# Second to fourth 512 rows of a down projection as seven half-size fp16 products, in a fused gated-attention kernel

## The chip, the core and the metric

One core of a Trainium2 chip runs the whole program. The metric is the device time of one execution in microseconds (us). Engines run their own instruction streams in order and meet through semaphores: TensorE (PE, with its weight loads PEld), VectorE (DVE), ScalarE (ACT), GpSimd (POOL) and SyncE (SP, which issues most DMAs).

## What is computed

```python
xn = layernorm(x)                                   # x: 2048 x 640
s  = windowed attention over the last 512 cached keys: 32 heads of 192, then @ wo
h  = sigmoid(xn @ w_gate) * (xn @ w_up)             # 640 -> 1536
g  = silu(h @ w_down)                               # 1536 -> 640, the down projection
out = x + s * g
```

The inputs are bf16. The change concerns `h @ w_down` and the silu behind it.

## The kernel before

**Stage B** comes first. It takes the 2048 rows in four groups of 512 (`s` = 0 to 3, L457). In each, `f` runs over the 12 blocks of 128 of the hidden size: ten matmuls of 512 columns give gate and up in the two banks of one PSUM pair (L469), ACT takes the sigmoid of the gate bank (L474), and DVE multiplies it with the up bank into `hT_sb[:, f, :]` (L475). Then the down projection takes the four row tiles `q` of 128: for every `f` a matmul of 512 columns and one of 128 with the same weights (L517), accumulated over the 12 blocks in one pair; ACT takes the sigmoid (L524), DVE multiplies (L525), POOL stores the tile `gB_sb` to `gB_d` (L541). PSUM is used as four pairs of banks that `bank2` (L79) hands out in turn, so a pair is free again when the group four steps back has been read.

**The other work of stage B** is put between these steps and runs in the order of the source, since the schedule is manual (L34). On DVE: layer norm statistics and normalization of the next 512 rows (L344, L349, L359); the sums of inputs for the query products (`sum_x`, L438 to L452); the scan of `wq` for its largest magnitude, sixteen pieces, each an `and` and a `max` (`scan_fold`, L199); the reduction to a scale (`set_scale`, L207), whose row maxima go to DRAM and come back on all partitions (two POOL DMAs), and `set_scale2` (L212), which waits for them. On ACT, in `s` = 3: the scaling of raw query weights to fp16 (`scale_raw`, L237) and copies (`copy_w`, L247); `sum_w` (L255) puts four DVE operations and one ACT copy in line, the copy waiting for DVE's second operation.

**Attention** follows (L548 on). Its first query products (`query_slots`, L579; L729) use PSUM banks 2 and 3, then 4 and 5, then 0, 1 and 6. The attention output goes through the output projection at the end, which already has the seven-product form (`product`, L933; `sum_op`, L706; `sum_quad`, L778): each 2x2 block product is made of seven products of half size and of sums before and after, where ACT copies partial results out of PSUM (`keep`, L944) and DVE adds (L957) or gates them (L921).

Of the kernel before, what the change touches and what calls it, by code (L numbers as in the profile page):

```python
# [17 lines left out]
def kernel(  # L18
# [14 lines left out]
    P = 128  # L33
# [53 lines left out]
    def flat(ps):  # L87
        return ps.rearrange("p b n -> p (b n)")
# [40 lines left out]
    w_sc = const.tile([P, 10], F32, name="w_sc")  # L129
# [141 lines left out]
    with ExitStack() as bctx:  # L271
# [3 lines left out]
        hpool = bctx.enter_context(tc.tile_pool(name="hpool", bufs=2))  # L275
# [14 lines left out]
        wmax = bone.tile([P, NCD, NSC], BF16, name="wmax")  # L290
        mx_row = bone.tile([P, P], F32, name="mx_row")
        x_tiles = {}

        def load_x(t):
            x_sb = xin_pool.tile([P, D], BF16, name=f"x_sb{t}")
            nc.sync.dma_start(x_sb[:], xf[t * P:(t + 1) * P, :])
            x_tiles[t] = x_sb[:]
# [157 lines left out]
        folds = {(0, 9): 0, (0, 10): 1, (0, 11): 2, (2, 0): 11, (2, 1): 12, (2, 2): 13, (2, 4): 14, (2, 5): 15}  # L455
        folds_q = {(0, q): 3 + q for q in range(TQ)} | {(1, q): 7 + q for q in range(TQ)}
        for s in range(NST):  # L457
            hT_sb = hpool.tile([P, NF, 512], BF16, name="hT_sb")
            pi = s // 2
            if s % 2 == 1:  # L460
                sw = swap(pi)
            for f in range(NF):
# [12 lines left out]
                nc.vector.tensor_tensor(hT_sb[:, f, :], gu[:, 1, :], sig_sb[:], ALU.mult)  # L475
# [11 lines left out]
                if (s, f) in folds:  # L487
                    scan_fold(wmax, folds[s, f])
                if s == 1 and f < NSB:
# [5 lines left out]
                elif s == 2 and f == 6:  # L495
                    set_scale(wmax[:].rearrange("p c n -> p (c n)"), mx_row)
# [16 lines left out]
            for q in range(TQ):  # L513
                oB_ps = flat(bank2())
                for f in range(NF):
                    for d0, dsz in d_chunks:
                        nc.tensor.matmul(  # L517
                            oB_ps[:, d0:d0 + dsz], lhsT=hT_sb[:, f, q * P:(q + 1) * P],
                            rhs=wd_sb[:, f, d0:d0 + dsz],
                            start=(f == 0), stop=(f == NF - 1),  # L520
                        )
                gB_sb = gpool.tile([P, D], BF16, name="gB_sb")
                sg = bone.tile([P, D], F32, name="sg")
                nc.scalar.activation(sg[:], oB_ps[:, 0:D], AF.Sigmoid)  # L524
                nc.vector.tensor_tensor(gB_sb[:], oB_ps[:, 0:D], sg[:], ALU.mult)  # L525
                if (s, q) in folds_q:
                    scan_fold(wmax, folds_q[s, q])
                if s == 3:
                    if q == 0:
                        scale_w(0, NCD - 1)  # L530
                    elif q < 3:
                        scale_raw(1, q - 1)
                    if q == 1:
                        sum_w(0, NCD - 1)
                        load_raw(1, 2, nc.gpsimd)
                    if q < 3:
                        sum_x(pi, 3 + q, sw)
# [531 lines left out]
```

## Time and profile before

| | |
|---|---|
| median of 3 runs | 881.0 us (880.94 to 881.07) |
| profiled execution | 881.17 us |
| its span in the profile | 879.4 us |
| PE busy | 872.0 us (99% of the span) |
| DVE / ACT / POOL busy | 670.0 / 577.2 / 231.6 us |
| L517, the down projection | 384 matmuls, 4 blocks of 13.04 us |
| granted TensorE clock in the first 220 us | 1.00 |

How to read it: the busy share of an engine is an average over stages with different limits. The chain of work that ended last follows the run back from its last instruction, at each step to what released it; in order of time it gives the start and length of each stretch. The lists of one engine in order of time give start, busy time, line, operation and operands, and in brackets the idle time before and what ended it. In the groups by form, the numbers behind the bar are the busy time in us, the mean ns of one, and idle time with what ended it.

### The profile page before, as it was taken

The numbers are of one execution on the slowest core, as the hardware profiler recorded it, in microseconds if no ns is written. First come the engines' busy times: TensorE is split into PE (matmuls) and PEld (weight loads), VectorE is DVE, ScalarE is ACT, GpSimd is POOL, SyncE is SP. The second block draws the span as 40 slices with busy tenths as digits, with TensorE's granted clock in tenths as the row PEclk, the third lists the DMA queues.
The fourth block names the chain that finished last, engine by engine and source line by source line (L and its number), as shares of the span: only waits on it lengthen the run. The fifth ranks groups of instructions, "written<-read, shape, count | busy, mean of one in ns | idle before, by whom it ended". The sixth has DMA issues, their size and how long they took to land.

```text
span 879.4 us, 18793 instructions
## 1 busy us (share of the span) xinstructions
PE 872.0 (99%) x7605; PEld 564.0 (64%) x7605; DVE 670.0 (76%) x1088; ACT 577.2 (66%) x693; POOL 231.6 (26%) x326
## 2 busy tenths in 40 slices
PE   9999999999999999999999999999999999999998
PEld 5445454557757757757757757757757777777775
DVE  4879947677767767767767767768877768888986
ACT  4323347765887887887797797786484666666662
POOL 0050212582344344334334334334000000000000
PEclk9999999999999999999999999999999999999999
DMA  9994465328698998898989898789997798557641
GB/s 273 268 276 113 107 117 123 93 56 156 163 218 143 197 215 151 178 225 150 196 210 143 200 213 154 147 193 215 215 272 137 203 367 267 181 168 267 193 138 38
DMA packets 246935, 161.34 MB, mean 183 GB/s; under 512 B 158848, under 2 KB 231808, under 8 KB 246848
## 3 DMA queue, kind: packets, MB, share of 16 engines
q1 hardware_dynamic: 238304, 132.90, 62.1%
q0 software_dynamic: 8544, 27.24, 14.4%
q8 instruction: 59, 0.97, 0.5%
q14 instruction: 28, 0.23, 0.1%
HBM read 93.65 MB, written 30.41 MB: 141 GB/s over the span
## 4 chain that ended last, share of the span: by engine, by line
PE 97%; ACT 1%; DVE 1%; DMA 0%; issue 0%; SPq 0%; DVEq 0%
PE ps_all L571 20%; PE ps_all L938 20%; PE ps_all L671 20%; PE ps_all L657 19%; PE ps_all L469 11%; PE ps_all L517 6%; PE ps_all L382 1%; ACT E L661 0%; DMA x_sb<-in_A_x_dram 0%; ACT qp L590 0%; DVE arm L921 0%; DVE arm L967 0%; ACT mid L720 0%; DVE arm L965 0%; DVE qT L605 0%
## 5 line engine op out<-in xcount | busy, mean ns | idle before, releaser
L661 ACT ACTIVATE E<-ps_all 128x1024 bf16<-128x1024 f32 x256 | 251.6, 1021 | 122.8 <-PE ps_all L657 122.1
L657 PE MATMUL ps_all<-qT,kT 64*128 64x512 bf16 x1536 | 197.7, 376 | 0.4 <-ACT E L661 0.3
L671 PEld LDWEIGHTS <-E 128*128 128x128 bf16 x2048 | 169.5, 98 | 9.9 <-issue 9.8
L671 PE MATMUL ps_all<-v_sb,E 128*128 128x193 bf16 x2048 | 174.9, 247 | 0.0
L605 DVE TENSOR_TENSOR qT<-ps_all,qp 128x512 bf16<-128x512 f32 x176 | 116.9, 687 | 47.5 <-PE ps_all L571 39.9
L592 DVE COPY qp<-ps_all 128x512 f32<-128x512 f32 x150 | 100.6, 687 | 48.0 <-PE ps_all L571 48.0
L657 PEld LDWEIGHTS <-kT 64*128 64x128 bf16 x1536 | 83.8, 94 | 80.2 <-issue 6.0
L678 DVE TENSOR_TENSOR o_st<-ps_all,rden 128x768 bf16<-128x768 f32 x128 | 122.5, 957 | 4.4
L938 PEld LDWEIGHTS <-mid 128*128 128x128 f16 x996 | 97.4, 98 | 37.8
L571 PE MATMUL ps_all<-mid,arm 64*128 64x512 f16 (+1 forms) x840 | 105.7, 376 | 0.0
L571 PE MATMUL ps_all<-mid 64*128 64x512 f16 (+1 forms) x840 | 104.5, 376 | 0.6 <-ACT qp L590 0.5
L571 PEld LDWEIGHTS <-mid 64*128 64x128 f16 x840 | 47.8, 94 | 45.0 <-issue 2.2
L571 PEld LDWEIGHTS <-arm 64*128 64x128 f16 x840 | 47.9, 94 | 43.8 <-issue 0.3
L774 ACT ACTIVATE mid<-mid,w_sc 128x1536 f16<-128x1536 bf16 x41 | 63.5, 1572 | 0.0
L971 POOL DMA_DIRECT2D out_dram<-arm x14 | 7.6, 542 | 196.3 <-DVE arm L967 196.3
L240 ACT ACTIVATE mid<-mid,w_sc 128x1536 f16<-128x1536 bf16 x37 | 58.2, 1572 | 0.6
L226 POOL DMA_DIRECT2D mid<-in_A_wq_dram x80 | 48.2, 608 | 23.9 <-DVE mid L262 22.4
L474 ACT ACTIVATE sig_sb<-ps_all 128x512 bf16<-128x512 f32 x48 | 28.0, 596 | 40.1 <-PE ps_all L469 37.1
L517 PE MATMUL ps_all<-wd_sb,hT_sb 128*128 128x512 bf16 (+1 forms) x384 | 52.8, 299 | 0.0
L938 PE MATMUL ps_all<-arm,mid 128*128 128x320 f16 x348 | 51.0, 299 | 0.0
L475 DVE TENSOR_TENSOR hT_sb<-ps_all,sig_sb 128x512 bf16<-128x512 f32 x48 | 32.5, 682 | 22.8 <-PE ps_all L469 11.7
L938 PE MATMUL ps_all<-op,mid 128*128 128x320 f16 x336 | 48.2, 299 | 0.0
(160 smaller groups left out, 1046.2 us busy)
## 6 DMA issues: line engine op xcount, KB each, us to landing
oT_d<-oT SPq DMA_DIRECT2D x64, 384.0 KB, 5.1
mid<-oT_d SPq DMA_DIRECT2D x45, 384.0 KB, 4.7
mid<-in_A_wq_dram POOLq DMA_DIRECT2D x80, 192.0 KB, 6.7
arm<-in_A_wo_dram SPq DMA_DIRECT2D x16, 480.0 KB, 5.7
v_sb<-in_A_v_cache_dram SPq DMA_DIRECT2D x28, 192.0 KB, 6.0
kraw<-in_A_k_cache_dram SPq DMA_DIRECT2D x26, 192.0 KB, 4.2
mid<-in_A_wq_dram POOLq DMA_DIRECT2D x9, 480.0 KB, 7.1
kT<-oT_d SPq DMA_DIRECT2D x11, 384.0 KB, 4.5
```

The lines of the kernel that those rows point to most:

```text
L240: nc.scalar.activation(raw.bitcast(F16), raw, AF.Copy, scale=w_up)
L469: nc.tensor.matmul(gu[:, i, :], lhsT=w[:, c, f * P:(f + 1) * P], rhs=xnT[s][:, c, :], start=(c == 0), stop=(c == NCD - 1),)
L517: nc.tensor.matmul(oB_ps[:, d0:d0 + dsz], lhsT=hT_sb[:, f, q * P:(q + 1) * P], rhs=wd_sb[:, f, d0:d0 + dsz], start=(f == 0), stop=(f == NF ...
L571: nc.tensor.matmul(ps_all[:, b, :], lhsT=w(r, c), rhs=x[r, c, :], start=(first and k == 0), stop=(k == len(cs) - 1), skip_group_check=True,)
L592: nc.vector.tensor_copy(dst, part(b))
L605: nc.vector.tensor_tensor(q_out(i, u, pp), part(b), t, ALU.add)
L657: nc.tensor.matmul(ps[:, b, :], lhsT=kT[h, c * PC + j, :], rhs=qT_t[r][i, j][h, pp, :], start=(j == 0), stop=(j == PC - 1),)
L661: nc.scalar.activation(E_t[r, i, pp][:, c, :, :], ps, AF.Exp, scale=scale_qk)
L671: nc.tensor.matmul(o_ps[:, q // 2, q % 2, 0:DH + 1], lhsT=E[:, c, h, q * P:(q + 1) * P], rhs=vt[:, c, 0:DH + 1], start=(c == 0), stop=(c = ...
L678: nc.vector.tensor_tensor(o_st[:, :, h * DH:(h + 1) * DH].rearrange("p (b i) d -> p b i d", b=2), o_ps[:, :, :, 0:DH], rden[:].to_broadcas ...
L774: eng.activation(t, t.bitcast(BF16), AF.Copy, scale=v_up)
L938: nc.tensor.matmul(ps_all[:, b, d0:d1], lhsT=a[:, c, :], rhs=w[:, c, d0:d1], start=(start and c == 0), stop=(c == KB - 1), skip_group_chec ...
```

## The change

`s` = 0 keeps its down projection. For `s` = 1 to 3, `down7` replaces the loop over `q`. h and `w_down` are held as fp16, scaled by powers of two. h is split in two halves of the hidden size and two pairs of row tiles, `w_down` in two halves of the hidden size and `LEFT` and `RIGHT` columns; for each of the two tiles of a pair, seven products of six matmuls of 320 columns are formed. Their operands need three new sums of `w_down` and one in place, made once (`sum_wd`), and three sums of h and one in place for every 512 rows (`sum_h`). Partial results are kept by ACT (`keep`); `gate` adds, takes the sigmoid with the joint scale undone and multiplies.

The scales come from bounds: ACT sums magnitudes (`Abs` with an accumulated output) of `w_up` (`scan_h`) and `w_down` (`scan_wd`), DVE takes the largest and cuts it to a power of two (`bound`), and a matmul with the identity spreads it over the partitions (`bound2`). `scan_abs` does so for pieces 7 to 15 of `wq`, in place of `scan_fold`.

`hT_sb` has one buffer instead of two. The first four x tiles are loaded into `h_sums`; `wmax` and the scans' output lie in the tiles of the `w_down` sums. What stood between the row tiles of `s` = 3 is now called from `after_down`.

```diff
-        hpool = bctx.enter_context(tc.tile_pool(name="hpool", bufs=2))
+        hpool = bctx.enter_context(tc.tile_pool(name="hpool", bufs=1))
...
+        NH = NF // 2
+        assert NSC * NCD == NH * DN and NH * DN == 3 * D
+        wd_sums = [bone.tile([P, NH, DN], F16, name=f"wd_t{n}") for n in range(3)]
+        h_sums = bone.tile([P, 3, NH, 2 * P], F16, name="h_sums")
+        halves = bone.tile([P, 8, DN], F32, name="halves")
+        wmax = wd_sums[1][:].bitcast(BF16).rearrange("p a b -> p (a b)").rearrange("p (c n) -> p c n", c=NCD)
+        scan_out = wd_sums[2][:].bitcast(BF16).rearrange("p a b -> p (a b)")
...
+        mx_b = bone.tile([P, P], BF16, name="mx_b")
+        scans = bone.tile([P, 20], F32, name="scans")
...
+        x_first = h_sums[:].bitcast(BF16).rearrange("p a b n -> p (a b n)")
...
+        def scan_abs(i):
+            nc.scalar.activation(scan_t[i], scan_t[i], AF.Abs, accum_out=scans[:, i - NSB + 1:i - NSB + 2])
+        def scan_h(k):
+            v = wu_sb[:, :, 3 * k * P:3 * (k + 1) * P]
+            nc.scalar.activation(
+                scan_out.rearrange("p (c n) -> p c n", c=NCD), v, AF.Abs, accum_out=scans[:, 10 + k:11 + k])
+        def scan_wd(k):
+            v = wd_sb[:, 3 * k:3 * (k + 1), :]
+            nc.scalar.activation(
+                scan_out.rearrange("p (c n) -> p c n", c=3), v, AF.Abs, accum_out=scans[:, 14 + k:15 + k])
+        def bound(mx, at):
+            nc.vector.tensor_reduce(mx, scans[:, at:at + 4], axis=mybir.AxisListType.X, op=ALU.max)
+            nc.vector.tensor_scalar(mx, mx, 1e-30, None, op0=ALU.max)
+            bits = mx.bitcast(I32)
+            nc.vector.tensor_single_scalar(bits, bits, 0x7F800000, op=ALU.bitwise_and)
+            nc.vector.tensor_copy(mx_b[:], mx.to_broadcast([P, P]))
+        def bound2(mx, ps, up, down, k):
+            nc.tensor.matmul(ps, lhsT=mx_b[:], rhs=ident[:], start=True, stop=True)
+            nc.vector.tensor_reduce(mx, ps, axis=mybir.AxisListType.X, op=ALU.max)
+            nc.vector.tensor_scalar(down, mx, k, None, op0=ALU.mult)
+            nc.vector.reciprocal(up, down)
...
+        def scale_wd(k):
+            v = wd_sb[:, 3 * k:3 * (k + 1), :]
+            nc.scalar.activation(v.bitcast(F16), v, AF.Copy, scale=wd_up)
+        def sum_wd(n):
+            B11, T1, T2, B21, T3, B22, T4 = wd_ops
+            a, b, c = ((T1, T3, B11), (T2, B22, T1), (T3, B22, T3), (T4, B21, T2))[n]
+            nc.vector.tensor_tensor(a, b, c, ALU.subtract)
+        def sum_h(h16, j0, j1):
+            A11, A21, A12, A22 = (
+                h16[:, k * NH + j0:k * NH + j1, i * 2 * P:(i + 1) * 2 * P] for k in range(2) for i in range(2))
+            S1, S2, S4 = (h_sums[:, n, j0:j1, :] for n in range(3))
+            tt = nc.vector.tensor_tensor
+            tt(S1, A21, A22, ALU.add)
+            tt(S2, S1, A11, ALU.subtract)
+            tt(S4, A12, S2, ALU.subtract)
+            tt(A21, A11, A21, ALU.subtract)
...
-        folds = {(0, 9): 0, (0, 10): 1, (0, 11): 2, (2, 0): 11, (2, 1): 12, (2, 2): 13, (2, 4): 14, (2, 5): 15}
-        folds_q = {(0, q): 3 + q for q in range(TQ)} | {(1, q): 7 + q for q in range(TQ)}
+        folds = {(0, 9): 0, (0, 10): 1, (0, 11): 2}
+        folds_a = {(1, 7): 7, (1, 8): 8, (1, 9): 9, (1, 10): 10, (1, 11): 11, (2, 0): 12, (2, 1): 13, (2, 3): 14,
+                   (2, 4): 15}
+        folds_q = {(0, q): 3 + q for q in range(TQ)}
+        wd16 = wd_sb[:].bitcast(F16)
+        wd_ops = [wd16[:, 0:NH, LEFT], wd_sums[0][:], wd_sums[1][:], wd16[:, NH:NF, LEFT], wd16[:, 0:NH, RIGHT],
+                  wd16[:, NH:NF, RIGHT], wd_sums[2][:]]
...
+        def after_down(s, q):
+            if s == 3:
+                if q == 0:
+                    scale_w(0, NCD - 1)
+                elif q < 3:
+                    scale_raw(1, q - 1)
+                if q == 1:
+                    sum_w(0, NCD - 1)
+                    load_raw(1, 2, nc.gpsimd)
+                if q < 3:
+                    sum_x(pi, 3 + q, sw)
+                else:
+                    load_k((1, 0), nc.gpsimd)
...
+        def down7(s, h16):
+            p0, p1, p2, p3 = ring
+            ring[:] = [p3, p0, p1, p2]
+            X, Z, Y = (2 * p0, 2 * p1), (2 * p0 + 1, 2 * p1 + 1), (2 * p2, 2 * p2 + 1)
+            A11, A21, A12, A22 = (
+                h16[:, k * NH:(k + 1) * NH, i * 2 * P:(i + 1) * 2 * P] for k in range(2) for i in range(2))
...
+            def half(n):
+                return halves[:, n, :]
...
+            def prod(p, b, a, n, start):
+                for j in range(NH):
+                    nc.tensor.matmul(
+                        ps_all[:, b, 0:DN], lhsT=a[:, j, p * P:(p + 1) * P], rhs=wd_ops[n][:, j, :],
+                        start=(start and j == 0), stop=(j == NH - 1), skip_group_check=True,
+                    )
...
+            def keep(b, n):
+                nc.scalar.activation(half(n), ps_all[:, b, 0:DN], AF.Copy)
...
+            def gate(q, d, b, n=None):
+                v = ps_all[:, b, 0:DN]
+                if n is not None:
+                    nc.vector.tensor_tensor(half(n), v, half(n), ALU.add)
+                    v = half(n)
+                sg = half(6 + sg_n[0] % 2)
+                sg_n[0] += 1
+                nc.scalar.activation(sg, v, AF.Sigmoid, scale=g_scale)
+                nc.vector.scalar_tensor_tensor(gB[q][:, d], v, g_scale, sg, op0=ALU.mult, op1=ALU.mult)
...
+            for p in range(2):
+                prod(p, X[p], A11, 0, True)
+                keep(X[p], p)
+            after_down(s, 0)
+            for p in range(2):
+                prod(p, Z[p], A12, 3, True)
+                gate(p, LEFT, Z[p], p)
+            after_down(s, 1)
+            for p in range(2):
+                prod(p, Y[p], S1, 1, True)
+                keep(Y[p], 2 + p)
+            for p in range(2):
+                prod(p, X[p], S2, 2, False)
+                keep(X[p], 4 + p)
+            after_down(s, 2)
+            for p in range(2):
+                prod(p, Y[p], S4, 5, False)
+                gate(p, RIGHT, Y[p], 4 + p)
+                store(p)
+            for p in range(2):
+                prod(p, X[p], A21, 4, False)
+                gate(2 + p, RIGHT, X[p], 2 + p)
+            after_down(s, 3)
+            for p in range(2):
+                prod(p, X[p], A22, 6, False)
+                gate(2 + p, LEFT, X[p])
+                store(2 + p)
...
-                nc.vector.tensor_tensor(hT_sb[:, f, :], gu[:, 1, :], sig_sb[:], ALU.mult)
+                if s == 0:
+                    nc.vector.tensor_tensor(hT_sb[:, f, :], gu[:, 1, :], sig_sb[:], ALU.mult)
+                else:
+                    nc.vector.scalar_tensor_tensor(
+                        h16[:, f, :], gu[:, 1, :], h_up, sig_sb[:], op0=ALU.mult, op1=ALU.mult)
+                    if f == NH + 3:
+                        sum_h(h16, 0, 4)
+                    elif f == NF - 1:
+                        sum_h(h16, 4, NH)
+                if s == 0 and f in (3, 6, 9, 11):
+                    scan_h((3, 6, 9, 11).index(f))
+                    if f == 11:
+                        bound(mx_h, 10)
+                elif s == 1:
+                    if f == 1:
+                        bound2(mx_w, flat(bank2())[:, 0:P], wd_up, wd_down, 1.0 / 4096)
+                        nc.vector.tensor_tensor(g_scale, h_down, wd_down, ALU.mult)
+                    elif 2 <= f < 6:
+                        scale_wd(f - 2)
+                    elif 6 <= f < 10:
+                        sum_wd(f - 6)
                 if s % 2 == 1 and f in sums[pi]:
                     sum_x(pi, sums[pi].index(f), sw)
...
                 if (s, f) in folds:
                     scan_fold(wmax, folds[s, f])
+                if (s, f) in folds_a:
+                    scan_abs(folds_a[s, f])
...
                 elif s == 2 and f == 6:
-                    set_scale(wmax[:].rearrange("p c n -> p (c n)"), mx_row)
+                    set_scale(scans[:, 0:10], mx_row)
                 elif s == 2 and f == NF - 1:
                     set_scale2(mx_row)
...
-            for q in range(TQ):
+            if s > 0:
+                down7(s, h16)
+            for q in range(TQ) if s == 0 else ():
                 oB_ps = flat(bank2())
...
+                if q == 1:
+                    bound2(mx_h, oB_ps[:, D:D + P], h_up, h_down, 0.25)
+                scan_wd(q)
                 gB_sb = gpool.tile([P, D], BF16, name="gB_sb")
-                sg = bone.tile([P, D], F32, name="sg")
-                nc.scalar.activation(sg[:], oB_ps[:, 0:D], AF.Sigmoid)
-                nc.vector.tensor_tensor(gB_sb[:], oB_ps[:, 0:D], sg[:], ALU.mult)
-                if (s, q) in folds_q:
-                    scan_fold(wmax, folds_q[s, q])
-                if s == 3:
-                    if q == 0:
-                        scale_w(0, NCD - 1)
-                    elif q < 3:
-                        scale_raw(1, q - 1)
-                    if q == 1:
-                        sum_w(0, NCD - 1)
-                        load_raw(1, 2, nc.gpsimd)
-                    if q < 3:
-                        sum_x(pi, 3 + q, sw)
-                    else:
-                        load_k((1, 0), nc.gpsimd)
+                sg = halves[:, 6:8, :].rearrange("p a n -> p (a n)")
+                nc.scalar.activation(sg, oB_ps[:, 0:D], AF.Sigmoid)
+                nc.vector.tensor_tensor(gB_sb[:], oB_ps[:, 0:D], sg, ALU.mult)
+                scan_fold(wmax, folds_q[s, q])
+                if q == TQ - 1:
+                    nc.vector.tensor_reduce(
+                        scans[:, 0:1], wmax.rearrange("p c n -> p (c n)"), axis=mybir.AxisListType.X, op=ALU.max)
+                    bound(mx_w, 14)
```

More of the change, by code (lines that the diff above doesn't have):

```diff
@@ L128 @@
     w_t = {0: w_even}
-    w_sc = const.tile([P, 10], F32, name="w_sc")
+    w_sc = const.tile([P, 17], F32, name="w_sc")
+    mx_h, h_up, h_down, mx_w, wd_up, wd_down, g_scale = (w_sc[:, i:i + 1] for i in range(10, 17))
     NWO, NVS = 16, 2 * NPAIR
@@ L201, in scan_fold @@
         v = scan_t[i]
-        bits = (wm[:] if i == 0 else v).bitcast(I32)
+        bits = (wm if i == 0 else v).bitcast(I32)
         nc.vector.tensor_single_scalar(bits, v.bitcast(I32), 0x7FFF7FFF, op=ALU.bitwise_and)
         if i > 0:
-            nc.vector.tensor_tensor(wm[:], wm[:], v, ALU.max)
+            nc.vector.tensor_tensor(wm, wm, v, ALU.max)
     def set_scale(wm, mx_row, mx=mx, n=0):
@@ L288 @@
         xnT = [x_even[0], x_odd, x_even[1], x_odd]
-        wmax = bone.tile([P, NCD, NSC], BF16, name="wmax")
+        NH = NF // 2
[4 more added lines that the diff above has]
+        wmax = wd_sums[1][:].bitcast(BF16).rearrange("p a b -> p (a b)").rearrange("p (c n) -> p c n", c=NCD)
@@ L291 @@
+        scan_out = wd_sums[2][:].bitcast(BF16).rearrange("p a b -> p (a b)")
         mx_row = bone.tile([P, P], F32, name="mx_row")
+        mx_b = bone.tile([P, P], BF16, name="mx_b")
+        scans = bone.tile([P, 20], F32, name="scans")
         x_tiles = {}
+        x_first = h_sums[:].bitcast(BF16).rearrange("p a b n -> p (a b n)")
         def load_x(t):
-            x_sb = xin_pool.tile([P, D], BF16, name=f"x_sb{t}")
-            nc.sync.dma_start(x_sb[:], xf[t * P:(t + 1) * P, :])
-            x_tiles[t] = x_sb[:]
+            x_tiles[t] = x_first[:, t * D:(t + 1) * D]
+            nc.sync.dma_start(x_tiles[t], xf[t * P:(t + 1) * P, :])
@@ new lines, with store @@
+        sg_n = [0]
+        def down7(s, h16):
[4 more added lines that the diff above has]
+                h16[:, k * NH:(k + 1) * NH, i * 2 * P:(i + 1) * 2 * P] for k in range(2) for i in range(2))
+            S1, S2, S4 = (h_sums[:, n, :, :] for n in range(3))
+            gB = {}
+            for q in range(TQ):
+                gB[q] = gpool.tile([P, D], BF16, name="gB_sb")
+            def half(n):
[17 more added lines that the diff above has]
+                nc.vector.scalar_tensor_tensor(gB[q][:, d], v, g_scale, sg, op0=ALU.mult, op1=ALU.mult)
+            def store(q):
+                t = s * TQ + q
+                nc.gpsimd.dma_start(gB_d[t * P:(t + 1) * P, :], gB[q][:])
+            for p in range(2):
[25 more added lines that the diff above has]
+                store(2 + p)
@@ L457 @@
         for s in range(NST):
             hT_sb = hpool.tile([P, NF, 512], BF16, name="hT_sb")
+            h16 = hT_sb[:].bitcast(F16)
             pi = s // 2
```

## Prediction, made before the changed kernel was run

> **What bounds the kernel now.** I read the page's chain first, then the chain of work in order of time, then DVE and ACT in order of time over the first 180 us, then the groups by form. The profiled execution took 881.17 us, 0.17 above the median of 881.0 (880.94 to 881.07); its span is 879.4, so 1.77 us lie outside it and I carry them unchanged. A difference over 0.2% (1.8 us) can be told from no change.
>
> ```profile
> PE 97%; ACT 1%; DVE 1%; DMA 0%; issue 0%; SPq 0%; DVEq 0%
> ```
>
> TensorE sets the end, so fewer columns through it can pay, as long as nothing else becomes late. Stage by stage (start, length):
>
> ```profile
> 34.96 13.04 PE ps_all L517 x96
> 48.00 25.90 PE ps_all L469 x120
> 73.90 13.04 PE ps_all L517 x96
> ...
> 151.78 13.04 PE ps_all L517 x96
> ```
>
> A stage of 512 rows is 25.90 us of gate/up matmuls (2.158 per f) and 13.04 us of down projection, without a gap. The engines behind it are not idle, though. This is DVE in the second 512 rows (s=1), from f=4 to f=11:
>
> ```profile
> 58.90 0.69 DVE L475 TENSOR_TENSOR hT_sb<-ps_all,sig_sb 128x512 bf16<-128x512 f32 x1 [1.47 <-PE ps_all L469]
> 59.51 1.47 DVE L442 TENSOR_TENSOR mid<-x_odd,mid 64x2560 f16<-64x2560 bf16 x1
> ...
> 74.51 0.69 DVE L475 TENSOR_TENSOR hT_sb<-ps_all,sig_sb 128x512 bf16<-128x512 f32 x1 [0.23 <-ACT sig_sb L474]
> ...
> 75.82 0.68 DVE L475 TENSOR_TENSOR hT_sb<-ps_all,sig_sb 128x512 bf16<-128x512 f32 x1
> ```
>
> Between 58.90 and the last h at 76.50 it waits 0.23 us in all. That h ends 2.6 us after TensorE has begun the down projection (73.90); this is harmless only because L517 needs h of f=11 last, 3.0 us into its first row tile. Whatever is put on DVE in this stretch makes h later one for one.
>
> **What the change removes.** 84 fp16 matmuls of 128x320 in place of 96. The last stage runs just this shape: its p5s evictions (L945) start at 798.55, 809.96 and 821.37, 11.41 us for 84, or 0.1358 each. So 3 x (13.04 - 11.41) = **4.9 us gained** if TensorE never waits. One product of six is 0.815.
>
> **What it adds, by these rows:**
>
> ```profile
> L957 DVE TENSOR_TENSOR acc<-ps_all,p1s 128x320 f32<-128x320 f32 x8 | 3.9, 491 | 7.6 <-PE ps_all L938 7.5
> L921 DVE SCALAR_TENSOR_TENSOR arm<-arm,w_sc 128x320 f32<-128x320 f32 x24 | 13.2, 552 | 0.8
> L945 ACT ACTIVATE p1s<-ps_all 128x320 f32<-128x320 f32 x16 | 7.0, 437 | 23.6 <-PE ps_all L938 23.6
> L710 DVE TENSOR_TENSOR arm<-mid,arm 128x1920 f16<-128x1920 f16 x4 | 4.6, 1148 | 0.0
> L716 ACT ACTIVATE arm<-arm 128x1920 bf16<-128x1920 bf16 x16 | 28.9, 1808 | 0.1
> ```
>
> Per gate: add 0.49, sigmoid, multiply 0.55. The sigmoid of 128x320 from SBUF is not in the trace: 0.44 (copy of that size) below, 0.70 (L524, 640 wide) above; I take 0.52, near the copy, plus what L240's scale operand seems to add. A scan on ACT is 1.8 + 0.2 (accumulator read). Each wd scaling is estimated at 1.9 from L240 (1.57 for 1536). For sum_h's two calls I interpolate f16 rows (0.35 for 384, 0.95 for 1536): 0.69 for 1024, 0.42 for 512, so 2.8 and 1.7 us with their chained waits (ends 1.4 and 4.6).
>
> *1. The order on DVE inside a gate.* The multiply waits for ACT's sigmoid and stands ahead of the next gate's add. The trace has such a pair:
>
> ```profile
> 122.36 0.70 ACT L524 ACTIVATE sg<-ps_all 128x640 f32<-128x640 f32 x1 [5.52 <-DVE gB_sb L525]
> ```
> ```profile
> 123.10 0.82 DVE L525 TENSOR_TENSOR gB_sb<-ps_all,sg 128x640 bf16<-128x640 f32 x1 [0.83 <-ACT sg L524]
> 124.75 0.82 DVE L525 TENSOR_TENSOR gB_sb<-ps_all,sg 128x640 bf16<-128x640 f32 x1 [0.83 <-ACT sg L524]
> ```
>
> One follows the other by 1.65 with 0.04 to 0.1 per hand-over. A gate is then 0.49 + 0.04 + 0.52 + 0.04 + 0.55 + 0.03 = 1.67 us of DVE, twice a product. Six gates have an add. A22 accumulates into the bank that the add of A21's gate reads, so it waits for that add. With DVE free, counting from the start of down: S4's gates begin at 7.4 and 9.05, A21's adds end at 11.2 and 12.9, A22's two products could start at 9.8 and start at 11.26 and 12.93. Stalls 1.5 + 0.9; a stage takes 13.7, **more than the 13.04 of before**. The gain is gone with this alone.
>
> *2. Start of s=1.* In s=0, ACT gets scans after f=3, 6, 9, 11 and in each row tile. The one after f=9 (2.0 us) stands before the sqrt table load that f=10's sigmoid follows: h of f=10 moves from 33.75 to 35.7; with DVE's fold, xn and fold behind it, h of f=11 ends at 39.6 instead of 37.6. TensorE wants it at 37.95: stall 1.7. DVE then does four gB and four folds with 1.6 us of bound work more than before, then a reduce of 128x1920 (2.1, as L208) and four small operations (0.8) before mx_b is there, at about 56.6. The matmul that spreads it stands behind f=1 of s=1, which ends at 54.1: stall 2.5. The spreading matmuls themselves cost 0.1 each. Together **+4.4**. Bounds: 0, if ACT and DVE regain their lag, to 7.
>
> *3. Late h in s=1.* DVE gains four wd sums (4.4), sum_h (2.8) and 0.05 per h (0.4) in the stretch that had 0.23 to spare; f=4's h starts at 63.35 and f=11's ends at 63.35 + 17.6 + 7.6 - 0.2 = 88.3. Gate/up ends at 78.3. A12 needs f=6 to 11, so its first product ends at 88.45 instead of 80.7: stall 7.75. The folds that left DVE in s=1 left its down part, which is behind this. DVE goes on with sum_h (1.7), sum_x (1.5), two xn (0.7): first add at 92.3, and the two A12 gates end near 95.6. S1's evictions stand behind their sigmoids on ACT, so S4 waits until 95.5: stall 2.8. Then A22's two, 1.5 + 0.9. Down takes 11.41 + 13.0 = 24.4: **+11.4**.
>
> *4. s=2.* Folds moved to ACT fit there (2.6 against 2.16 per f, with f=2 free). The scale's round trip by DMA keeps its 12.8 us (107.7 to 120.48): DVE stands in it until 30.9 us into the stage, the first add is then 2.5 late, S4 waits 1.75 for S1's evictions, A22 2.4. Down 15.6: **+2.6** (0.7 if the trip is shorter).
>
> *5. s=3.* ACT's copy for the query weights stands ahead of the sigmoids of f=10 and 11 and waits for a DVE sum:
>
> ```profile
> 150.80 0.52 ACT L245 ACTIVATE mid<-mid 64x384 f16<-64x384 f16 x1 [1.42 <-DVE mid L259]
> 151.34 1.09 ACT L474 ACTIVATE sig_sb<-ps_all 128x512 bf16<-128x512 f32 x2
> ```
>
> sum_h (2.8) is queued before that sum, so h of f=11 ends 4.4 us after gate/up: A12 stalls 2.15. Between A11 and S4, ACT also has scale_w (2.6) and scale_raw (1.6), DVE sum_h (1.7), sum_x (1.5) and two gates: S1's banks are read at 13.0 instead of 8.65, stall 4.35. Two more sum_x (3.0) and sum_w (1.5) precede S4's gates: A22's first waits 3.4, its second 0.9. Down 22.2: **+9.2** (bounds 0.7 and 12). DVE's own work here (14 gate operations 7.3, sum_h 1.7, sum_w 1.5, sum_x 4.5 = 15.0) exceeds 13.04 whatever the waits.
>
> *6. Entry into attention.* Its first products use banks 2 and 3; bank 2 is now the last product's. They wait for sigmoid and multiply: **+1.45** (none before, where the last tile was in banks 0 and 1).
>
> Other moves: h in one buffer costs nothing (TensorE is a whole f ahead when it is rewritten); the x loads into h_sums, POOL's stores and scan loads and SP's transposes have microseconds of cover in the longer stages.
>
> **Sum.** 4.4 + 11.4 + 2.6 + 9.2 + 1.45 = +29.0: 881.17 + 29.0 = **910** us.
>
> **A rule against it.** In this trace the granted clock stays 1.00 through the longest wait behind the warm-up (1.95 us at 172.6); no long idle stretch is shown. The Trainium skill, "TensorE: Matmul & The Clock Gate", Part 1, has the clock halved after an idle window of about 3.4 us, for about as long. By it, an estimate: two of the stalls above reach it, and the sum would be 911 to 913.
>
> **The rivals.**
> - *Evictions keep up* (faster): stalls vanish if the waits of A22 and S4 end before TensorE arrives; needs gates under 0.82 us of DVE and h on time. 881.2 - 4.9 + up to 1.45 = 876 to 878. Against it: 0.49 + 0.55 alone exceed 0.82. Chance 0.06; within 0.2%: 0.03.
> - *Only the gate order costs*: 3 x 0.7 + 1.45 = +3.6, with step 2 +8: 885 to 889, up to 896. Needs h late by under 2 us in s=1 and 3; DVE without gaps in the fence speaks against it. Chance 0.09.
> - *More than summed* (long idle or slower shared engines): 921 to 930. Chance 0.05.
> - *Forecast*: 896 to 921, from the bounds of the sigmoid (18 gates, -0.08 to +0.18 each), sum_h (ends over s=1 and s=3: -3 to +5) and steps 2 and 5. Chance 0.77.
>
> The range 893 to 921 takes part of the second rival in (0.8). Faster 0.06, same 0.03, slower 0.91.
>
> **What would show it.** Down 24, 15.6 and 22 us in the chain by time; A12's loads waiting for hT_sb from DVE; S4's for ACT's halves; A22's for DVE's add; mx_b's matmul waiting about 2.5; DVE without gaps from f=4 of s=1. Wrong if down stages show 11.4, or if DVE shows idle time before h of f=11.

## The result and the profile after

The changed kernel takes **914.6 us** (median of 6 runs, 912.3 to 921.7) against 881.0 of the kernel before (880.8 to 881.1, 6 runs): slower, ratio 1.0396 with a 95% interval of 1.0358 to 1.0435. The predicted 910 lay 4.6 us below, the range 893 to 921 held it. The profiled execution took 914.7 us with a span of 912.9; all terms below are from it.

The chain of work that ended last, from the page of the changed kernel (shares of the span):

```profile
PE 83%; DVE 6%; SPq 4%; ACT 3%; DMA 2%; issue 2%; DVEq 0%; ACTq 0%
```

TensorE held 97% of the chain before. Where it lost its hold is seen in its own list in order of time (start, busy time, line, operation, operands; in brackets the idle time before and what ended it):

```profile
39.20 3.71 PE L685 MATMUL ps_all<-wd_sb,hT_sb 128*128 128x512 bf16 x26 [1.50 <-DVE w_sc L322]
...
56.46 0.23 PE L330 MATMUL ps_all<-ident,mx_b 128*128 128x128 bf16 x1 [2.66 <-DVE mx_b L326]
56.52 1.24 PE L613 MATMUL ps_all<-x_odd,wg_sb 128*128 128x512 bf16 x5
57.60 2.26 PE L613 MATMUL ps_all<-x_odd,wu_sb 128*128 128x512 bf16 x5
59.66 1.96 PE L613 MATMUL ps_all<-x_odd,wg_sb 128*128 128x512 bf16 x5
...
88.35 0.45 PE L550 MATMUL ps_all<-wd_sb,hT_sb 128*128 128x320 f16 x1 [5.66 <-DVE hT_sb L622]
89.72 2.05 PE L550 MATMUL ps_all<-wd_sb,hT_sb 128*128 128x320 f16 x7 [0.92 <-DVE hT_sb L622]
91.56 5.23 PE L550 MATMUL ps_all<-wd_t,h_sums 128*128 128x320 f16 x24
...
101.52 0.97 PE L550 MATMUL ps_all<-wd_t,hT_sb 128*128 128x320 f16 x6 [1.43 <-DVE halves L561]
103.16 0.97 PE L550 MATMUL ps_all<-wd_t,hT_sb 128*128 128x320 f16 x6 [0.67 <-DVE halves L561]
...
138.39 1.79 PE L550 MATMUL ps_all<-wd_sb,h_sums 128*128 128x320 f16 x12 [1.84 <-ACT halves L556]
...
184.82 1.79 PE L550 MATMUL ps_all<-wd_sb,h_sums 128*128 128x320 f16 x12 [2.33 <-ACT halves L556]
186.44 1.79 PE L550 MATMUL ps_all<-wd_sb,hT_sb 128*128 128x320 f16 x12
191.14 3.30 PE L550 MATMUL ps_all<-wd_t,hT_sb 128*128 128x320 f16 x12 [2.90 <-DVE halves L561]
195.64 0.61 PE L733 MATMUL ps_all<-mid 64*128 64x512 bf16 x4 [1.20 <-DVE gB_sb L566]
```

Each named wait is there: for the last h of s=0 (39.20; the bracket names `w_sc`, the next operation on DVE, but h ends at 39.15), for the row maximum `mx_b` (56.46), for late h (88.35), for ACT's evictions (138.39, 184.82), for DVE's add in front of A22 (101.52, 191.14), and at the entry of attention (195.64). Three lines show what the sum left out: after the wait of 2.66 us the five matmuls at 57.60 take 2.06 us to the next start, and those at 59.66 take 1.79, where 1.08 is usual; and 24 matmuls at 91.56 take 5.11 where 3.26 is usual. The granted clock is 0.72 from 56 to 62 us and 0.50 from 88 to 94.

DVE in the second 512 rows, the counterpart of the list of before, at its end:

```profile
84.42 0.68 DVE L352 TENSOR_TENSOR hT_sb<-hT_sb 128x1024 f16<-128x1024 f16 x1
85.02 1.15 DVE L342 TENSOR_TENSOR wd_t<-wd_sb,wd_t 128x1920 f16<-128x1920 f16 x1
86.09 1.48 DVE L505 TENSOR_TENSOR mid<-mid,x_odd 64x2560 f16<-64x2560 bf16 x1
87.50 0.16 DVE L408 RECIPROCAL rstd<-rstd 128x4 f32<-128x4 f32 x1
87.58 0.71 DVE L622 SCALAR_TENSOR_TENSOR hT_sb<-ps_all,w_sc,sig_sb 128x512 f16<-128x512 f32 x1
88.22 0.79 DVE L414 TENSOR_SCALAR xn<-x_sb,mv,rstd 128x640 bf16<-128x640 bf16 x2
88.93 0.73 DVE L622 SCALAR_TENSOR_TENSOR hT_sb<-ps_all,w_sc,sig_sb 128x512 f16<-128x512 f32 x1
```

No gap stands between these, and h of the last f ends at 89.66, where gate/up had ended at 79.96. The new operations, from the groups by form of the first 196 us (behind the bar: busy us, mean ns of one):

```profile
L565 ACT ACTIVATE halves<-halves,w_sc 128x320 f32<-128x320 f32 x18 | 10.1, 562 | 23.5 <-DVE halves L561 23.5
L566 DVE SCALAR_TENSOR_TENSOR gB_sb<-halves,w_sc 128x320 bf16<-128x320 f32 x18 | 9.9, 551 | 11.9 <-ACT halves L565 11.9
L561 DVE TENSOR_TENSOR halves<-ps_all,halves 128x320 f32<-128x320 f32 x18 | 8.7, 485 | 1.8 <-PE ps_all L550 1.7
L337 ACT ACTIVATE wd_sb<-wd_sb,w_sc 128x1920 f16<-128x1920 bf16 x4 | 7.6, 1893 | 0.0
```

| stage (us) | before | after | lost | predicted |
|---|---|---|---|---|
| start of s=1 and its gate/up, end at | 73.90 | 79.96 | 6.06 | 4.4 |
| down, s=1 | 13.04 | 24.17 | 11.13 | 11.4 |
| down, s=2 | 13.04 | 15.82 | 2.78 | 2.6 |
| down, s=3 | 13.04 | 22.70 | 9.66 | 9.2 |
| entry into attention | 0 | 1.19 | 1.19 | 1.45 |
| from the first attention matmul to the end of the span | 714.6 | 717.3 | 2.7 | 0 |

### The profile page after: what moved, and what is told of

Same layout as the page of the kernel before. It is cut to its first block, busy times and chain, and to the rows that moved or that the text cites. A ratio compares the mean times of both kernels' runs of the same rounds, so it can differ in the third digit from the quotient of the medians.

```text
span 912.9 us, 18848 instructions
## 1 busy us (share of the span) xinstructions
PE 877.0 (96%) x7558; PEld 569.4 (62%) x7571; DVE 686.9 (75%) x1144; ACT 624.0 (68%) x761; POOL 230.8 (25%) x326
## 4 chain that ended last, share of the span: by engine, by line
PE 83%; DVE 6%; SPq 4%; ACT 3%; DMA 2%; issue 2%; DVEq 0%; ACTq 0%
PE ps_all L1100 19%; PE ps_all L733 19%; PE ps_all L833 19%; PE ps_all L819 17%; PE ps_all L613 7%; PE ps_all L550 2%; SPq L198 1%; SPq L372 1%; ACT E L823 1%; DMA kraw<-in_A_k_cache_dram 1%; DVE halves L561 1%; ACT halves L565 1%; DMA mid<-in_A_wq_dram 1%; DVE wd_t L206 1%; SPq L853 0%
## 5 line engine op out<-in xcount | busy, mean ns | idle before, releaser
L839 DVE RECIPROCAL rden<-ps_all 128x4 f32<-128x4 f32 x128 | 23.3, 182 | 29.5 <-PE ps_all L833 27.6
L1100 PE MATMUL ps_all<-mid 128*128 128x320 f16 x312 | 44.8, 299 | 0.0
L618 ACT ACTIVATE sig_sb<-ps_all 128x512 bf16<-128x512 f32 x48 | 28.0, 595 | 23.7 <-PE ps_all L613 22.7
```

The lines of the kernel that those rows point to most:

```text
L1100: nc.tensor.matmul(ps_all[:, b, d0:d1], lhsT=a[:, c, :], rhs=w[:, c, d0:d1], start=(start and c == 0), stop=(c == KB - 1), skip_group_chec ...
```

## The experiments

**My theory** after the result: all of it is order. Every wait has a cause in what stands ahead of the awaited operation on DVE or ACT, and nothing is lost for lack of engine time. **The rival**: DVE and ACT have too much work in these stages whatever its order, so undoing one wait only shows the next. Runs 1 to 7 have one time each, 8 to 10 an interval.

**1. Adds ahead of multiplies.** Edits are to the changed kernel.

```diff
+            def add(b, n):
+                nc.vector.tensor_tensor(half(n), ps_all[:, b, 0:DN], half(n), ALU.add)
...
                 prod(p, Y[p], S4, 5, False)
-                gate(p, RIGHT, Y[p], 4 + p)
-                store(p)
+                add(Y[p], 4 + p)
             for p in range(2):
                 prod(p, X[p], A21, 4, False)
-                gate(2 + p, RIGHT, X[p], 2 + p)
+                add(X[p], 2 + p)
+            for p in range(2):
+                gate(p, RIGHT, Y[p], 4 + p, True)
+                store(p)
+            for p in range(2):
+                gate(2 + p, RIGHT, X[p], 2 + p, True)
```

> Edit: in the seven-product down projection the four adds of S4's and A21's gates stand in DVE's queue ahead of the four multiplies that wait for ACT; nothing else moves. Theory (the order in DVE's queue makes A22 wait): A22's waits of 2.1, 2.1 and 2.9 us in s=1, 2 and 3 go, so the three down stages fall from 24.2, 15.8 and 22.7 to about 22.1, 13.7 and 19.8; the gates' tail then ends later and the entry into attention waits about 2.5 instead of 1.2; net about -6 us at the start of attention. Rival (the amount of work on DVE and ACT decides, not its order): the three stages stay within 0.5 of what they were, as the same operations run on the same engines.

Measured: 910.88 us; attention starts 4.9 us earlier, at 190.78. TensorE's list of this kernel, end of s=1 (A21, then A22):

```profile
98.03 1.79 PE L550 MATMUL ps_all<-wd_sb,hT_sb 128*128 128x320 f16 x12
99.66 1.79 PE L550 MATMUL ps_all<-wd_t,hT_sb 128*128 128x320 f16 x12
```

The brackets in front of A22 are gone here and in s=2, and of 2.90 in s=3 0.47 is left, so its waits were the order inside the gates. In s=2 the gain was taken back: S4 waited 3.20 instead of 1.84, as an xn buffer became free later (a DMA, 1.87 us of wait on DVE), and the stage took 16.5 where 13.7 was expected.

**2. The sums of w_down on POOL.**

```diff
-            nc.vector.tensor_tensor(a, b, c, ALU.subtract)
+            nc.gpsimd.tensor_tensor(a, b, c, ALU.subtract)
```

> Edit: the four sums of w_down run on POOL instead of DVE. Theory (h of s=1 is late because DVE's queue is full): h of f=11 ends 4.4 us earlier, A12's waits in s=1 fall from 7.0 to about 2.6, and its down stage from 24.2 to about 20. Rival (ACT holds h back, with its scans and table loads between the sigmoids): f=10's and f=11's sigmoids stay where they are and h gains less than 1.5 us. A second rival (POOL slows DVE): DVE's 16-bit operations get longer while POOL adds, and the gain is under 3.

Measured: 922.39 us, attention starts 8.4 us later. POOL's list and DVE's list of this kernel:

```profile
69.08 4.18 POOL L342 TENSOR_TENSOR wd_t<-wd_sb,wd_t 128x1920 f16<-128x1920 f16 x1
```
```profile
69.51 0.73 DVE L622 SCALAR_TENSOR_TENSOR hT_sb<-ps_all,w_sc,sig_sb 128x512 f16<-128x512 f32 x1
70.27 4.34 DVE L499 TENSOR_TENSOR mid<-x_odd,x_sw 64x2560 f16<-64x2560 bf16 x1
```

While POOL subtracts, DVE's 16-bit sum of two SBUF inputs takes 4.34 us (3.3 to 4.3 in all four) where it takes 1.49 alone (1.48 and 1.49 for the two later ones in this run); the h beside it, which reads PSUM, keeps 0.70 to 0.75. Four operations of 1.15 us left DVE, and four others grew by 1.8 to 2.9 us each: the second rival held, and nothing was gained. All four end 1.33 to 1.35 us behind the end of a POOL subtraction (here 74.61 and 73.26), which reads as if each stood until POOL's was done and then ran. The Trainium skill, "GPSIMD Engine Reference", section 1 (Specifications), states that POOL shares its SBUF interfaces with VectorE, with contention for instructions that have two SBUF inputs; these lines agree and give the size.

**3. The bound ahead of the 2.15 us reduction.**

```diff
-                    nc.vector.tensor_reduce(
-                        scans[:, 0:1], wmax.rearrange("p c n -> p (c n)"), axis=mybir.AxisListType.X, op=ALU.max)
                     bound(mx_w, 14)
+                    nc.vector.tensor_reduce(
+                        scans[:, 0:1], wmax.rearrange("p c n -> p (c n)"), axis=mybir.AxisListType.X, op=ALU.max)
```

> Edit: the reduction of 128x1920 at the end of s=0 stands behind the bound of w_down in DVE's queue instead of ahead of it. Theory (queue order): the matmul that spreads the scale waits 0.5 us instead of 2.66. If the halved clock that follows it (f=2 and f=3 of s=1 take 1.7 us more together) is caused by that wait, it goes as well and s=1 begins f=4 3.9 us earlier; if the clock falls for another reason, 2.2 us earlier. Rival (ACT's scans set when the scale is ready): the wait stays above 2.

Measured: 913.12 us. TensorE's list of this kernel:

```profile
54.37 0.23 PE L330 MATMUL ps_all<-ident,mx_b 128*128 128x128 bf16 x1 [0.47 <-DVE mx_b L326]
80.53 0.31 PE L550 MATMUL ps_all<-wd_sb,hT_sb 128*128 128x320 f16 x1 [2.16 <-DVE hT_sb L622]
86.50 0.45 PE L550 MATMUL ps_all<-wd_sb,hT_sb 128*128 128x320 f16 x1 [5.66 <-DVE hT_sb L622]
```

The wait of 2.66 falls to 0.47 and the clock stays whole, so gate/up of s=1 ends 3.8 us earlier (76.18). But h of the last f is late for its own reason, and TensorE, arriving sooner, waits 8.74 instead of 6.97 for it; half of the gain is left at the end of the stage (102.30 against 104.13), and none at the start of attention (196.16 against 195.64): in s=2 S4 waits 3.31 instead of 1.84, behind an xn DMA again (1.98 us on DVE), and the clock halves after it.

**4. sum_x of the first half moved from s=1 to s=2** (six DVE operations of 1.48 us each).

```diff
-        sums = (4, 5, 6, 7, 9, 11), (2, 4, 7)
+        sums = (0, 1, 2, 3, 4, 5), (2, 4, 7)
...
-                if s % 2 == 1 and f in sums[pi]:
-                    sum_x(pi, sums[pi].index(f), sw)
+                if s > 1 and f in sums[s - 2]:
+                    sum_x(s - 2, sums[s - 2].index(f), sw)
```

> Edit: the six sums of inputs of the first two groups of rows stand in s=2 (f=0 to 5) instead of s=1. Theory (DVE's queue in s=1): 8.9 us leave the stretch in which h is late, so h of f=11 is bound by ACT's sigmoid behind a scan and a table load, about 4 us after gate/up ends instead of 9.7; A12's waits fall from 7.0 to 1.5, the down stage of s=1 from 24.2 to about 16 or 17, and gate/up of s=2 stays at 25.9 (h and a sum take 2.25 us per f there against 2.16). Rival (DVE is only short of time in total over stage B): what s=1 gains, s=2 loses, so the start of attention moves less than 3 us.

Measured: 908.68 us. Down in s=1 takes 18.0 instead of 24.2; its waits for h are 0.70 and 1.58, and the second now ends behind ACT (two table loads and two scans ahead of the last sigmoid), not DVE. In s=2 down grows from 15.8 to 18.2, behind this line of DVE's list:

```profile
130.44 0.45 DVE L414 TENSOR_SCALAR xn<-x_sb,mv,rstd 128x640 bf16<-128x640 bf16 x1 [2.88 <-DMA x_odd<-xn]
```

Attention starts 3.6 us earlier, hardly more than the 3 that the rival allowed. Late h in s=1 was DVE's queue, as predicted. So far the rival could still be right: each cure had brought up another wait.

**5. s=3 back to 96 matmuls**, on the scaled fp16 operands.

```diff
-            if s > 0:
+            if s in (1, 2):
                 down7(s, h16)
+            for q in range(TQ) if s == 3 else ():
+                oB_ps = flat(bank2())
...
+                        nc.tensor.matmul(
+                            oB_ps[:, d0:d0 + dsz], lhsT=h16[:, f, q * P:(q + 1) * P],
+                            rhs=wd16[:, f, d0:d0 + dsz],
```

> Takes the fourth 512 rows (s=3) back to 96 matmuls with whole-tile gates, on the scaled fp16 operands (T3 is turned back by one DVE subtraction at f=1 of s=3; the sums of h are left out there). Theory: the stage's 22.7 us come from the sums of h, the order of the gates and ACT's and DVE's query work between them, so they go back to 13.0 to 13.2, and the wait of 1.2 at the entry of attention goes: attention starts at 195.6 - 9.6 - 1.2 = 184.8, in all 902 to 906. Rival, that the work for the query weights in s=3 is late for itself (h of f=11 behind ACT's copy) whatever the product's form: a wait of 2 us or more stays ahead of the last blocks of the first row tile, 905 to 909.

Measured: 904.59 us. From the chain in order of time of this kernel (start, length):

```profile
172.68 2.99 PE ps_all L688 x22
175.68 10.22 PE ps_all L688 x74
185.91 7.77 PE ps_all L752 x70
```

The stage takes 13.23, attention follows without a gap. The same scaled work for the query weights stands in ACT's and DVE's queues, and 96 matmuls hide it: the loss of 10.85 in s=3 belongs to the seven products and their sums in that place.

**6. 96 matmuls in all stages**; scales, scans and the single buffer of h stay.

```diff
-                    if f == NH + 3:
-                        sum_h(h16, 0, 4)
-                    elif f == NF - 1:
-                        sum_h(h16, 4, NH)
...
-                    elif 6 <= f < 10:
-                        sum_wd(f - 6)
...
-            if s > 0:
-                down7(s, h16)
+            for q in range(TQ) if s > 0 else ():
```

> The 96 matmuls of before in all stages, on operands scaled to fp16: bounds, scans, scalings, the single buffer for h and the scans of wq on ACT stay; the sums of w_down and of h and the seven products are left out. Theory: only the start of s=1 is left, 4.4 us and 1.7 of halved clock: attention starts at 164.8 + 6.1 = 171, in all 886 to 889. Rival, that h in one buffer, the scalings on ACT or the moved scans cost on their own (my step on the single buffer said nothing): TensorE waits appear in s=1 to s=3 too, 890 or more.

Measured: 892.21 us, more than the theory's 886 to 889. TensorE's list of this kernel:

```profile
56.36 0.23 PE L330 MATMUL ps_all<-ident,mx_b 128*128 128x128 bf16 x1 [2.67 <-DVE mx_b L326]
56.42 1.24 PE L613 MATMUL ps_all<-x_odd,wg_sb 128*128 128x512 bf16 x5
57.50 1.24 PE L613 MATMUL ps_all<-x_odd,wu_sb 128*128 128x512 bf16 x5
...
83.88 10.23 PE L677 MATMUL ps_all<-wd_sb,hT_sb 128*128 128x512 f16 x74 [1.82 <-DVE hT_sb L622]
...
173.78 8.88 PE L741 MATMUL ps_all<-mid 64*128 64x512 bf16 x80 [1.80 <-DVE gB_sb L685]
```

Three things in one run. The start costs 4.3, but the clock stays whole behind the same wait. h is still late in s=1 (0.72 and 1.82), by two scans and a table load that stand ahead of ACT's last sigmoids, which I had given no price there. And the entry wait of 1.80 stays with no product of mine behind it: the spreading matmul takes one turn of the four pairs (`bank2`), so the last tile lies in another pair than before. The rival's "on their own" was right by 4.3 us. A wait in attention (1.86 at 342.82) explains most of the rest.

**7. A version against all these waits.** Adds ahead of multiplies; A12's sigmoids behind the evictions and written into the output tile; `sum_h` in one piece behind the last h; scans, layer norm and `sum_x` moved to where DVE's and ACT's lists had gaps; one more xn buffer; s=3 as in 5. Some of the lines:

```diff
-        sums = (4, 5, 6, 7, 9, 11), (2, 4, 7)
+        sums = {(2, 0): (0, 0), (2, 1): (0, 1), (2, 2): (0, 4), (2, 7): (0, 2), (2, 10): (0, 3), (3, 5): (0, 5),
+                (3, 2): (1, 0), (3, 4): (1, 1), (3, 7): (1, 2)}
...
+            def sig(q, d, v):
+                nc.scalar.activation(gB[q][:, d], v, AF.Sigmoid, scale=g_scale)
...
+                    n = f - (5, 3, 3)[s]
+                    if 0 <= n < TQ:
+                        ln_stats(t + n)
```

> A version against all the waits found, for s=1 and s=2 alone in seven products: adds ahead of multiplies, sigmoids behind the evictions and written as bf16 into the output tile, the sums of h in one piece behind h of f=11, the scan of s=0's f=6 and f=9 at f=5 and f=8, the 2.15 us reduction and the spreading matmul one f later, layer norm two f earlier, sum_x of the first half in s=2, the wait for the scale's row behind the gates of s=2, one more xn buffer; s=3 as in the run beside it. Theory, that all of the loss is order and not the amount of work: down 11.4 to 13 in s=1 and s=2, start of s=1 within 1 us of before: 877 to 883. Rival, that DVE and ACT have too much work in s=1 and s=2 whatever the order: waits of 3 us or more stay in one of them, 886 to 895.

Measured: 889.35 us, but attention starts at 165.80, only 1.0 later than before: down is 12.9 us in s=1 and 12.35 in s=2. The time lies in the rival's range, but not for its reason: no wait in s=1 or s=2 exceeds 1.28 us, and 7.2 us were lost later, in attention. TensorE's list and, in the next fence, the chain there:

```profile
599.29 12.27 PE L859 MATMUL ps_all<-v_sb,E 128*128 128x193 bf16 x112 [4.00 <-DVE qT L793]
```
```profile
586.39 11.02 DMA kraw<-in_A_k_cache_dram
597.40 0.02 issue
597.43 0.42 DVE k_sb L164
```

A k load lands 11.0 us after its issue, the scaling that waits for it holds DVE's queue, and 112 matmuls behind the wait take 12.27 instead of 9.49, at a granted clock of 0.50 from 599 to 605 us.

**8. The remaining waits (a), and the k load earlier (b).** a: the last scaling of `w_down` on DVE, statistics and `sum_wd` one f earlier, and in s=3 `sum_w` ahead of the sigmoid of its f. b: as a, with the k load moved (the second diff).

```diff
+                            nc.vector.tensor_scalar(v.bitcast(F16), v, wd_up, None, op0=ALU.mult)
```

```diff
-            if k == 2 and g > 0:
-                load_k((g + 1, 0))
...
+            elif k == 9 and g + 2 < NG:
+                load_k((g + 2, 0))
```

> The version against all waits, second try. In the first, TensorE still waited 1.28 (s=1), 0.72 (s=2) and 1.53 us (s=3) for h of the last f. In s=1 ACT had been the slower engine from f=3 on (1.9 + 0.58 us per f, then two table loads): the last scaling of w_down now runs on DVE, the statistics and the sums of w_down come one f earlier. In s=2 one sum_x moves from f=10 to f=8 and the scans end at f=5. In s=3 ACT's copy waited 1.48 us in each of four places for a DVE sum queued behind h: the sums now stand ahead of that f's sigmoid. Theory (order, not amount): the three waits go, down 11.4 to 11.9 in s=1 and s=2, 13.04 in s=3, attention starts at 165.8 - 3.5 = 162.3 against 164.8 before, in all 878 to 880 if the later parts are as in the kernel before, with 2 to 7 us more where a k load lands late in attention. Rival: a wait of over 1 us stays in a stage, 881 or more even without late k loads.

> As the run beside it, and in attention the load of the next group's first k tile is issued some 9 steps earlier, right behind the scaling that frees its buffer and ahead of the v loads on SP's queue. In the first version TensorE waited 4.0 us at 599.3 for a k load that landed 11.0 us after its issue, and its clock dropped behind it. Theory, that the time which all versions lose in attention is this load's lack of slack: no wait for kraw is left, 878 to 880 in every run. Rival, that the load is late for the traffic beside it, wherever it is issued: waits for kraw or for another load stay, and runs differ by 2 us or more.

Measured: a **879.55** us (878.5 to 883.0 in 10 runs), ratio to before 0.9976 (0.9957 to 0.9996); b **877.91** us (877.7 to 878.4 in 10 runs), ratio 0.9953 (0.9933 to 0.9973). TensorE's list of b, s=1 from A11 on:

```profile
73.35 3.42 PE L550 MATMUL ps_all<-wd_sb,hT_sb 128*128 128x320 f16 x24
76.61 3.42 PE L550 MATMUL ps_all<-wd_t,h_sums 128*128 128x320 f16 x24
79.87 1.79 PE L550 MATMUL ps_all<-wd_sb,h_sums 128*128 128x320 f16 x12
81.50 1.79 PE L550 MATMUL ps_all<-wd_sb,hT_sb 128*128 128x320 f16 x12
83.13 1.79 PE L550 MATMUL ps_all<-wd_t,hT_sb 128*128 128x320 f16 x12
84.76 1.24 PE L624 MATMUL ps_all<-mid,wg_sb 128*128 128x512 bf16 x5
```

No bracket is left, and 73.35 to 84.76 is the 11.41 that the matmuls alone take; s=2 shows the same. The waits for the k loads (1.7 us of DVE's time in a) are gone in b, and so is the spread between runs: those loads had lacked slack. In s=1 and s=2, then, the rival is wrong: the same products run there without a wait, with the other work placed elsewhere.

**9. The control**: all of version b, but 96 matmuls in every stage, without the sums of h and of w_down, the last tile in banks 0 and 1. The edit is to version b.

```diff
-            if s in (1, 2):
-                down7(s, h16)
-            for q in range(TQ) if s == 3 else ():
+            if s == 3:
+                bank_order[:] = [2, 3, 1, 0]
+            for q in range(TQ) if s > 0 else ():
```

> The control to the version that beat both kernels: all of its order of work, its scalings, its early k load, but 96 matmuls in every stage; the sums of w_down and of h are left out, and the last row tile gets banks 0 and 1, as in the kernel before. Theory, that the seven products are worth what the matmuls say, 2 x (13.04 - 11.41) = 3.26, once nothing waits, and the new order nothing by itself: 877.9 + 3.3 = 881.2, within 0.2% of before. Rival, that the version gains by its new order or its early k load and not by the products: 877.5 to 879.

Measured: 880.98 us (880.7 to 881.3, 12 runs), ratio to before 0.9987 (0.9971 to 1.0004). With the last tile back in its banks no wait is left at the entry of attention, which bears out the reading of run 6. The new order, scales and early load bring nothing that can be told from no change; the products bring 880.98 - 877.91 = 3.07, near the 3.26 that two stages can save (timed apart, each beside the kernel before; by the two ratios it is 3.0).

**10. Seven products in s=3 too, in version b** (a; b with two `sum_x` behind attention's first additions and four copies on POOL).

```diff
-            p0, p1, p2, p3 = ring
+            p0, p1, p2, p3 = ring if s < 3 else (3, 0, 2, 1)
```

> The version that beat both kernels with seven products in s=3 as well: ACT's and DVE's query work moved out of that stage's down projection (the fifth piece's scaling and sums at f=8 and f=9, four sum_x in gate/up, two behind the gates), the products in pairs of banks that attention asks for last. Theory (order, not amount): another 1.63, 876.3. Rival, that DVE's work in s=3 is too much for the stage whatever the order (my step 5 counted 15.0 us for its down projection alone): TensorE waits 1 us or more there or at the entry into attention, 877.5 to 881.

> The version with seven products in s=3 too, second try. The first lost 1.57 us to sigmoids late on ACT and 2.71 behind two sum_x that stood ahead of attention's first additions on DVE. Now four of ACT's copies in s=3 go to POOL, the two scalings for attention stand behind the first evictions and behind the last sigmoids, and the two sum_x behind attention's first three additions. Theory (order, not amount): both waits go, 877.9 - 1.6 = 876.3. Rival (DVE is full in s=3): waits of 1 us or more stay there or move a few us into attention, 877.5 or more; POOL's copies may add to it, as POOL's work slowed DVE's 16-bit operations in the run with the sums of w_down there.

Measured: a 882.73 us (ratio 1.0007, 0.9994 to 1.0020), with these waits in TensorE's list:

```profile
151.16 2.60 PE L550 MATMUL ps_all<-wd_sb,hT_sb 128*128 128x320 f16 x18 [1.11 <-ACT sig_sb L638]
...
168.47 7.07 PE L753 MATMUL ps_all<-mid 64*128 64x512 f16 x49 [2.71 <-DVE qT L787]
```

b 877.58 us (877.5 to 877.8), ratio 0.9962 (0.9948 to 0.9976). In b the stage takes 11.4 without a wait and attention starts 1.2 us earlier than in the version with two stages, but waits of 0.41 and 0.73 and slower first products, behind the `sum_x` that moved there, give it back by 171 us. Here the rival holds in part: in both versions DVE's work of s=3 was moved, not hidden. The two versions were timed apart, and their difference of 0.3 us is not settled.

## Why the prediction was right, and where it was not

*Which way, and how much.* Slower by 33.5 us in the profiled execution, 29.0 predicted. All five places were named, and without the halved clock at the start each total lies within 0.5 us of the measured one, in steps 3 to 5 partly with other terms or reasons. The missing 4.5 are that clock (1.7) and attention (2.7 in all from its start on, 2.4 of it in two waits behind k loads, 2.14 at 496.05 and 0.23 at 562.00), which no step had.

*Step 1, the order inside a gate.* Right: A22 waits 1.43 + 0.67 in s=1 and s=2 (predicted 1.5 + 0.9), and run 1 removed them by order alone. The sigmoid measured 0.56, where 0.52 was taken from the bounds 0.44 and 0.70.

*Step 2, start of s=1.* Right: 1.50 and 2.66 (1.7 and 2.5). Run 3 confirmed the reduction as the cause of the second, and showed that this wait was not worth its length: h of the last f held the stage in any case. A sum of stalls counts each as if the next did not depend on it.

*Step 3, late h in s=1.* The mechanism was right (run 4) and the sum too (24.2 against 24.4), but with other terms: 6.97 of waits for h (7.75), and no wait at S4 where I had 2.8. In its place the clock halved behind the 5.66 and cost about 3 us; while TensorE ran at half rate, ACT's evictions caught up. That the total fits is partly chance.

*Step 4.* The sizes were right: S4 1.84 (1.75), A22 2.10 (2.4). The reason for S4 was not. DVE's list of the changed kernel:

```profile
134.03 0.45 DVE L414 TENSOR_SCALAR xn<-x_sb,mv,rstd 128x640 bf16<-128x640 bf16 x1 [0.51 <-DMA x_odd<-xn]
134.39 0.28 DVE L214 TENSOR_REDUCE w_sc<-mx_row 128x1 f32<-128x128 f32 x1
135.35 0.49 DVE L561 TENSOR_TENSOR halves<-ps_all,halves 128x320 f32<-128x320 f32 x1
```

DVE does not stand in the scale's round trip: its second DMA was issued at 129.06 and landed 4.3 us later, and DVE came to the row only at 134.39, without a wait. It was held by the sums of h and by xn, which waited for SP's transposes to free its buffer, so "0.7 if the trip is shorter" does not hold. That the first add came about when forecast, 31.2 us into the stage against 30.9, is luck. The prediction gave these transposes microseconds of cover; in the changed kernel and runs 1 to 6 the wait for them is 0.5 to 2.9 us.

*Step 5, s=3.* The total was right (22.7 against 22.2); A12 2.19 (2.15), S4 2.33 (4.35), A22 2.90 (4.3), and again a halved clock for the difference. DVE's 15.0 us of work in that stage was the sound reason: run 10 moved it and did not hide it.

*Step 6, entry.* 1.20 (1.45), but the reason was only half of it: run 6 has 1.80 without seven products, since the spreading matmul turns the ring of pairs.

*Other moves.* That h in one buffer costs nothing holds in runs 8 and 9, where no wait stands at any stage's start. ACT's work in s=1 was given no price: in run 6 it makes h 2.5 us late there without any product. In the changed kernel DVE was later still, so the sum did not show it.

*The rule on the clock* stood outside the sum, as +1 to +3. It belonged in it: the clock cost 1.7 at the start, and some 3 us each in s=1 and s=3, where it took the place of waits. The row that it was held against is no wait of TensorE: over the 1.95 us at 172.6 the chain lists DVE and ACT, while TensorE's own list has brackets of 0.31 and 0.23 there. The kernel before had no long wait to judge by.

*The first rival* (evictions keep up, 876 to 878) was rightly thought unlikely for this kernel. Its argument, that 0.49 + 0.55 exceed 0.82, is wrong as a bound: A12's, S4's and A21's multiplies can stand behind the adds, and then only the adds must keep pace. Run 8 has that in two stages, at 877.9, and run 10 b in three, at 877.6.

*Open*: why the k loads, for which DVE does not wait in the profile of the kernel before, become late in attention in the changed kernel and runs 1 to 8 a (0.4 to 5.1 us of DVE's waits). Run 8 shows that earlier issue cures it, not what in the first 200 us sets it off. Nor is it known what spreads the changed kernel over 912.3 to 921.7, or the kernel before over 880.5 to 888.5 in the series beside runs 8 to 10: of each one execution was profiled.

## What to carry to other kernels

A product form that saves 1.6 us per stage must be paid in its order: evictions that free a bank go ahead of the arithmetic that only makes output, and every operation put ahead of a late one on a full queue costs its length. Price the waits first, then ask of each what would be late next if it went; single cures of order gained 1.5 to 6 us here (one of placement lost 8); all together, with s=3 back on 96 matmuls (10 of it by run 5) and the k load earlier, they gained 37. Measure the gain against a control with the same order and the old products, or a reordering will be taken for it.

## What the hardware showed beyond expectation

- **The clock falls behind waits shorter than expected, and not always.** Behind the same wait of 2.66 to 2.67 us at 56 us, the granted clock was 0.72 from 56 to 62 us in five kernels (the changed one, runs 1, 2, 4 and 5) and 1.00 in run 6. Half rate began between 0.3 us ahead of the restart and 1.2 behind it and lasted some 3.4 us (0.28 of 6 us, doubled). In s=3 of the changed kernel two waits of 1.84 and 0.35 us were enough (0.50 from 178 to 180 us, and 24 matmuls at 177.61 are busy for 4.88 us instead of 3.42), while one of 1.84 at 138.39 was not. The Trainium skill, "TensorE: Matmul & The Clock Gate", Part 1, has about 3.4 us of idle, in a window that runs freely; that it may or may not happen fits a free window, that 2.66 us or less are enough does not.
- **POOL's elementwise work holds up DVE's two-input 16-bit sums**: 3.3 to 4.3 us instead of 1.49, each ending 1.33 to 1.35 us behind POOL's (run 2); operations that read PSUM keep their time.
- **One k load of 192 KB took 11.0 us to land** in run 7, where the median of all loads into that buffer is 3.6.
